# Dealing the weight conversion out as 6, 10, 9 and 7 pieces over the first four units of a gated attention and MLP kernel

## The chip, the core and the metric

The kernel runs on one core of one Trainium2 chip. The metric is device time in microseconds (us) for one execution. The engines are named TensorE (PE in the profile, with PEld for its weight loads), VectorE (DVE), ScalarE (ACT), GpSimd (POOL) and SyncE (SP, which issues the transfers). Each engine works through its own instructions strictly in order. An instruction that must wait for another engine holds up everything behind it on its own engine.

## What is computed

The first half is a gated linear recurrence over 4 batches, 8 heads, 768 tokens and a head size of 48. The second half is an MLP with a quick GELU over the 3072 tokens, with 384 features and 2048 hidden columns. The MLP weights arrive as 64-bit floats.

```python
f = 1.0 / (1.0 + np.exp(-f_logit))
for t in range(S):
    state = f[:, :, t, :, None] * state + np.einsum('bhd,bhe->bhde', k[:, :, t], v[:, :, t])
    y[:, :, t] = np.einsum('bhd,bhde->bhe', q[:, :, t], state)
x = y.transpose(0, 2, 1, 3).reshape(B * S, H * D)
h = x @ w_in
out = (h * (1.0 / (1.0 + np.exp(-1.702 * h)))) @ w_out
```

## The kernel before

**Units.** The tokens are cut into twelve units of 256 tokens, 0 to 11. `attention(n)` returns the parts of unit n's recurrence. In units 0 to 2 there are six levels ("W" parts, `level`), two transposes of the keys ("T", `turn_k`), the chain of states ("S", lines 511 to 544), and a last part that multiplies by the states and sends the result to the MLP's layout (line 546 on, `to_x`). That last part of a unit is put at the head of the next unit's first part, so it lies at the seam between the two. Three "begin" parts ("B", "K") of the next unit are put between them.

**One level.** On TensorE a level has 32 score products (`sc`, L384) and then, for the level before, 32 products with the values (`y`, L448). VectorE follows with two multiplications that carry keys and queries to the next level in place in X (L436, L437) and one masked copy of the scores out of PSUM to A (L410). ScalarE copies the keys of the next level aside (`Kc`, L423). The next level's scores need A copied (they reuse its PSUM tile), Kc copied and X carried on; VectorE's multiplication needs the scores to have been read. So one level waits for the one before, from TensorE to VectorE and back. From unit 3 on, two levels are done at once (L439 in place of L436 and L437), and VectorE turns the inputs (L327) where TensorE (`t`, L339) does it for units 0 to 2. GpSimd multiplies the gates together (`tot`, L376).

**The chain of states.** At the end of a unit VectorE computes four states, one after the other (`st`, L538, L540, L543). The products of the last part (`y`, L563) need them, and the next unit's first scores need the last L543, since it reads the same PSUM tile.

**Weights.** Lines 146 to 241 turn the 64-bit weights into 32-bit ones. There are 32 pieces of 128 by 384 numbers, in 16 pairs. Pairs come in groups of four: two of `w_in` and then two of `w_out`, which serve four of the sixteen blocks of 128 hidden columns. A pair is fetched by SyncE into one of three buffers (`bits`, L180). It is begun by two ScalarE instructions (`a`, L208). Then it takes ten VectorE instructions, two each of L223, L219, L226, L227 and L228; the two pieces of a pair alternate, and L228 writes the finished weight. Each `convert()` issues one of these ten; a new pair is begun when at most five are left over. When a pair is finished, the fetch of the third pair after it is issued, in the order of SyncE's queue at that moment.

**What sets the order.** `merge` walks through a unit's parts and puts two things between them: MLP work for TensorE (`fill`), shared out by columns, and conversion instructions for VectorE, shared out by `pieces`. A call with `pieces=8` issues 8 times NOP = 40 of them, in proportion to weights of the parts: three for each W and T and one for each B in units 0 and 1, three for W and S and one for T and B from unit 2 on. `by=0.7` in the fourth call brings them all within the first 70% of the weights. Four conversions are issued before unit 0, so 4 + 5 (8 + 10 + 8 + 6) are 164, and there are 160 to do. `some` holds an MLP block back in the order while the pieces it needs are not yet finished in program order.

```python
n_ops = min(int(pieces * NOP * at_ops / (by * total_ops)), pieces * NOP) - ops
while fill and done < end and fill[0][2] <= ready:
```

Unit 0 has no MLP work. Instead of it `keep_up` (L809) gives TensorE products that nobody reads: two in each of the first three levels of unit 0, and three in the first level of unit 1. They are in both kernels. Unit 1 has the MLP of unit 0 beside it, unit 2 that of units 0 and 1, unit 3 that of units 0 to 2. The order on all engines is the program's up to `fill_order.close()`; behind it that holds for TensorE only.

**MLP blocks.** `h` (L727) is the first matrix product. ScalarE's sigmoid `sg` (L732) and VectorE's `g` (L733) follow it, and `o` (L755) is the second product. It is added up over four groups by L791 (ScalarE) and L793 (VectorE). From unit 3 on, `mlp_unit` uses sums of weights (`T`, L622) in the second product (L704). All MLP products, transposes (`t` L339, `tkn` L505) and turned values (`tv` L284) share four PSUM tiles named `mm`.

Of the kernel before, what the change touches and what calls it, by code (L numbers as in the profile page):

```python
# [23 lines left out]
def kernel(  # L24
# [206 lines left out]
    def convert():  # L231

        if state["begin"] < len(pairs) and len(todo) <= NOP:
            begin_pair(state["begin"])
            state["begin"] += 1
        if todo and todo[0]:
            todo.pop(0)()
        if todo and todo[0] is None:
            todo.pop(0)
            state["done"] += 2  # L240
            fetch_weights()
# [556 lines left out]
    def mlp_blocks(*blocks):  # L798

        hs, os = zip(*(mlp_block(n, r) for n, r in blocks))  # L800
        return sum(hs, []) + sum(os, [])
# [10 lines left out]
    LAG = 18 * DM  # L812

    def parts_of(n):

        parts = list(units[n][1])
        _, inter = parts.pop()
        if n:
            kind, scores = parts[0]
            _, ahead = units[n - 1][1][-1]  # L820
            parts[0] = kind, lambda: (ahead(), scores())
        if n < N_TURN:

            def with_v(l):
                kind, fn = parts[l]
                return kind, lambda: (fn(), load_vl(n, l) if n == 0 or l else None, keep_up(2 * (n == 0 and l < 3) or 3 * (n == 1 and l == 0)))
            parts[:NL] = [with_v(l) for l in range(NL)]
        if n + 1 < NALL:
            begin_f, begin, begin_k, begin_gates = units[n + 1][0]
            i = len(parts)  # L830
            if n + 1 < N_FILL:

                parts.append(("K", lambda: (begin_k(), begin_gates(), load_vl(n + 1, 0) if n + 1 < N_TURN else None)))
                parts.insert(i - 4, ("B", begin))
                parts.insert(i - 5, ("B", begin_f))
            else:
                kind, states = parts.pop()
                parts += [("B", begin_k), (kind, lambda: (states(), begin_gates()))]
                parts.insert(i - 3, ("B", lambda: (begin_f(), begin())))
        else:  # L840
            parts.append(("W", inter))
        return parts

    def merge(n, fill, columns, share, pieces=0, hold=0, by=1.0, chores=()):

        parts = parts_of(n)
        total = sum(share(kind) for kind, _ in parts)
        converting = {"W": 3, "T": 3, "B": 1} if n < N_FILL - 1 else {"W": 3, "V": 4, "S": 3, "T": 1, "B": 1}  # L850
        total_ops = sum(converting.get(kind, 0) for kind, _ in parts)
        held = sum(share(kind) for kind, _ in parts[:hold])
        at = at_ops = done = ops = 0
        for kind, fn in parts:
            ready = state["done"]
            fn()
            for chore in chores[:2]:
                chore()
            chores = chores[2:]
            at += share(kind)  # L860
            at_ops += converting.get(kind, 0)
            n_ops = min(int(pieces * NOP * at_ops / (by * total_ops)), pieces * NOP) - ops
            ops += n_ops
            first, n_columns = done, max(0, columns * (at - held) / (total - held) - done)

            def some(end):
                nonlocal done
                while fill and done < end and fill[0][2] <= ready:
                    w, emit, _ = fill.pop(0)
                    emit()  # L870
                    done += w
            for i in range(n_ops):
                some(first + n_columns * i / n_ops)
                convert()
            some(first + n_columns)
# [4 lines left out]
    UNIT = NFF * NK * U + U // P * NFF * DM  # L880
# [12 lines left out]
        load_raw(1, j)  # L893
    load_vn(1)
    fill = []
    merge(0, fill, 0, steady, 8)
    fill += mlp_blocks((0, 0)) + mlp_blocks((0, 1))
    merge(1, fill, UNIT // 2 - LAG // 2, steady, 10, hold=1)
    fill += mlp_blocks((1, 0), (1, 1)) + mlp_blocks((0, 2), (1, 2))
    merge(2, fill, UNIT, steady, 8)  # L900
    fill += mlp_blocks((2, 0), (2, 1)) + mlp_blocks((2, 2), (0, 3)) + mlp_blocks((1, 3), (2, 3))
    merge(3, fill, 3 * UNIT // 2 - LAG // 2, steady, 6, by=0.7)
    fill_order.close()
    for n in range(3, NALL):
        fill += mlp_unit(n)
# [33 lines left out]
```

## Time and profile before

| what | value |
|---|---|
| median of 8 runs | 659.58 us (657.49 to 662.04) |
| the profiled execution's own time | 656.95 us |
| its span | 654.8 us |
| mean granted TensorE clock | 0.997 |
| TensorE busy | 635.4 us, 97% |
| VectorE busy | 444.9 us, 68% |
| ScalarE busy | 229.7 us, 35% |
| GpSimd busy | 54.7 us, 8% |

Times in the trace are counted from the start of the span. Unit 0's levels begin at 13.1 us, unit 1's first scores are at 44.64 us, unit 2's at 85.20 us, unit 3's at 142.13 us. From 212 us on, units 4 to 11 and the rest of the MLP run with no conversion. A tenth of busy time on the page is one slice of 16.4 us. Where an instruction's duration overlaps the next one on the same engine, the distance from start to start is what it costs.

### The profile page before, as it was taken

The page shows a single profiled execution, that of the slowest core. Times are in us where ns is not written, and L with a number is a line of the kernel's source. Part 1 is how long each engine was busy: PE and PEld are TensorE (multiplying, and loading weights), DVE is VectorE, ACT ScalarE, POOL GpSimd, SP SyncE. Part 2 cuts the span into 40 slices and gives each one's busy share as a digit, 9 for nine tenths or more (in the row PEclk, how much of TensorE's full clock was granted, in tenths as well). Part 3 has the DMA queues.
Part 4 walks back from the last instruction along what each step waited for, and adds up shares of the span by engine and source line. Part 5 has one row for each costly group of instructions (what it writes and reads, how often), then busy time and mean ns, then how long its engine had stood idle before and what let it go on. Part 6 is the DMA issues. An engine that isn't in the chain of part 4 may idle for free.

```text
span 654.8 us, 20407 instructions
## 1 busy us (share of the span) xinstructions
PE 635.4 (97%) x8964; PEld 544.8 (83%) x8964; DVE 444.9 (68%) x802; ACT 229.7 (35%) x477; POOL 54.7 (8%) x116
## 2 busy tenths in 40 slices
PE   6979999999999999999999999999999999999997
PEld 5656767767678689989989989989989989989997
DVE  2999878788787658658558558558559557553571
ACT  3464443233224324324324324324324333222120
POOL 3020020010001002002002002002002002000000
PEclk9999999989999999999999999999999999999999
DMA  8887975384034535514614615605604202101000
GB/s 191 225 203 181 226 167 134 96 208 84 25 81 133 155 85 121 153 39 119 162 30 121 158 35 123 164 26 127 160 27 106 65 25 63 38 2 26 25 1 24
DMA packets 67554, 67.67 MB, mean 103 GB/s; under 512 B 30410, under 2 KB 61290, under 8 KB 67466
## 3 DMA queue, kind: packets, MB, share of 16 engines
q1 hardware_dynamic: 67466, 66.38, 40.7%
q8 instruction: 70, 1.15, 0.8%
q14 instruction: 18, 0.15, 0.1%
HBM read 56.92 MB, written 8.65 MB: 100 GB/s over the span
## 4 chain that ended last, share of the span: by engine, by line
PE 86%; DVE 8%; ACT 2%; issue 1%; DMA 1%; SPq 0%; DVEq 0%; ACTq 0%
PE h L727 37%; PE o_Y L704 8%; PE o L755 7%; PE o_X L704 7%; PE o_Z L704 7%; PE sc L384 5%; PE y L448 5%; PE o_W L704 4%; PE t L339 2%; PE y L563 2%; PE sc L523 1%; PE tkn L505 1%; DVE s L219 1%; DMA xT<-yT 1%; DVE A L410 1%
## 5 line engine op out<-in xcount | busy, mean ns | idle before, releaser
L727 PE MATMUL h<-xT,w_in 128*128 128x256 f32 (+1 forms) x1152 | 259.4, 381 | 4.1 <-DMA xT<-yT 2.5
L727 PEld LDWEIGHTS h<-xT,w_in 128*128 128x128 f32 x1152 | 216.0, 190 | 36.3 <-issue 3.1
L733 DVE TENSOR_TENSOR g<-h,sg 128x256 f32<-128x256 f32 (+1 forms) x192 | 80.9, 423 | 97.5 <-ACT sg L732 95.1
L732 ACT ACTIVATE sg<-h 128x256 f32<-128x256 f32 (+1 forms) x192 | 73.3, 383 | 191.8 <-PE h L727 187.2
L423 ACT COPY Kc<-X 128x512 f32<-128x512 f32 x69 | 46.2, 669 | 120.8 <-DVE X L439 84.8
L755 PE MATMUL o<-w_out,g 128*128 128x384 f32 x192 | 67.4, 499 | 0.0
L439 DVE TENSOR_TENSOR X<-X,tot 128x1024 f32<-128x1024 f32 x45 | 55.1, 1224 | 15.3 <-PE sc L384 10.2
L755 PEld LDWEIGHTS o<-w_out,g 128*128 128x128 f32 x192 | 35.8, 193 | 23.3 <-issue 2.4
L704 PE MATMUL o_X<-w_out,g 128*128 128x192 f32 x288 | 51.9, 329 | 0.0
L704 PE MATMUL o_Y<-T,S 128*128 128x192 f32 x288 | 51.2, 331 | 0.0
L704 PEld LDWEIGHTS o_Y<-T,S 128*128 128x128 f32 x288 | 46.5, 190 | 2.5 <-DVE u L679 1.2
L704 PEld LDWEIGHTS o_X<-w_out,g 128*128 128x128 f32 x288 | 47.3, 190 | 0.8
L410 DVE TENSOR_TENSOR A<-sc,masks 128x512 f32<-128x512 f32 x72 | 46.8, 680 | 0.0
L448 PE MATMUL y<-A,vl 64*48 64x64 f32 x2304 | 41.2, 217 | 0.2
L376 POOL TENSOR_TENSOR tot<-F 128x512 f32<-128x512 f32 x12 | 12.5, 1040 | 327.5 <-DVE st L540 327.5
L448 PEld LDWEIGHTS y<-A,vl 64*48 64x48 f32 x2304 | 36.2, 120 | 3.7 <-issue 3.3
L327 DVE STREAM_TRANSPOSE X<-raw 128x1024 f32<-128x1024 f32 x18 | 36.7, 2039 | 2.4 <-PE y L563 2.0
L571 ACT COPY yT<-y 48x512 f32<-48x512 f32 x48 | 27.8, 580 | 13.6 <-PE y L563 13.0
L384 PEld LDWEIGHTS sc<-X,Kc 48*64 48x64 f32 x1344 | 24.4, 136 | 9.0 <-ACT vl L288 3.1
L384 PE MATMUL sc<-X,Kc 48*64 48x64 f32 x1344 | 28.6, 222 | 2.2 <-DVE A L410 1.9
L376 POOL TENSOR_TENSOR tot<-tot 128x256 f32<-128x256 f32 (+4 forms) x60 | 27.4, 457 | 4.7
L704 PE MATMUL o_Z<-w_out,g 128*128 128x192 f32 x144 | 26.6, 332 | 0.0
(93 smaller groups left out, 660.9 us busy)
## 6 DMA issues: line engine op xcount, KB each, us to landing
vl<-v_tok SPq DMA_DIRECT2D x60, 192.0 KB, 2.8
bits<-in_moe_w_out_dram SPq DMA_DIRECT2D x8, 768.0 KB, 9.9
bits<-in_moe_w_in_dram SPq DMA_DIRECT2D x8, 576.0 KB, 7.5
v_tok<-in_v_dram SPq DMA_DIRECT2D x10, 384.0 KB, 4.3
vn<-v_tok SPq DMA_DIRECT2D x10, 384.0 KB, 6.6
xT<-yT SPq DMA_DIRECT2D x24, 144.0 KB, 2.8
raw<-in_f_logit_dram SPq DMA_DIRECT2D x18, 192.0 KB, 4.2
raw<-in_q_dram SPq DMA_DIRECT2D x18, 192.0 KB, 4.1
```

What stands on the lines that cost most here:

```text
L327: nc.vector.transpose(out.rearrange("p (a i j) -> p a j i", a=NP, j=R), raw[:, j].rearrange("p a (j d) -> p (a j) d", j=R)[:, :, :32],)
L376: nc.gpsimd.tensor_tensor(tn, t2[:, :, 0], t2[:, :, 1], ALU.mult)
L384: nc.tensor.matmul(out[g * HS:(g + 1) * HS, h, a, :], lhsT=lhs(h, a * U + g * G), rhs=rhs(h, a * U + g * G), start=True, stop=True,)
L410: nc.vector.tensor_tensor(A[:, :, c:c + w].rearrange("p h (x t) -> p h x t", t=64), t["sc"][:, :, c:c + w].rearrange("p h (x t) -> p h x t ...
L423: nc.scalar.copy(c.rearrange("p (n m) -> p n m", m=m), X[:, j, :NA].rearrange("p (n two m) -> p n two m", two=2, m=m)[:, :, hf, :],)
L439: nc.vector.tensor_tensor(qk, qk, by, ALU.mult)
L448: nc.tensor.matmul(dst(h, g, a), lhsT=vls[n, u][g * 64:(g + 1) * 64, (2 * a + h) * D:(2 * a + h + 1) * D], rhs=A(h, g, a), start=(start an ...
L704: nc.tensor.matmul(t[bank], lhsT=lhs(f), rhs=rhs(f), start=(new and f == 0), stop=(f == HF - 1), skip_group_check=True,)
L727: nc.tensor.matmul(ph, lhsT=w_in[:, c, ff * P:(ff + 1) * P], rhs=xTs[n][:, c, :], start=(c == 0), stop=(c == NK - 1))
L732: nc.scalar.activation(sg, ph, AF.Sigmoid, scale=1.702)
L733: nc.vector.tensor_tensor(g[ff // FG][:, ff % FG, :], ph, sg, ALU.mult)
L755: nc.tensor.matmul(t["po"], lhsT=g[ff // FG][:, ff % FG, tt * P:(tt + 1) * P], rhs=w_out[:, ff, :], start=(ff == ffs[0]), stop=(ff == ffs[ ...
```

## The change

The `pieces` of three of four calls of `merge` change, for units 0, 2 and 3. Units 0 to 3 were dealt 8, 10, 8 and 6 pieces; they are dealt 6, 10, 9 and 7 after it. Both add up to 32. The products that nobody reads are not touched.

```diff
-    merge(0, fill, 0, steady, 8)
+    merge(0, fill, 0, steady, 6)
     fill += mlp_blocks((0, 0)) + mlp_blocks((0, 1))
     merge(1, fill, UNIT // 2 - LAG // 2, steady, 10, hold=1)
     fill += mlp_blocks((1, 0), (1, 1)) + mlp_blocks((0, 2), (1, 2))
-    merge(2, fill, UNIT, steady, 8)
+    merge(2, fill, UNIT, steady, 9)
     fill += mlp_blocks((2, 0), (2, 1)) + mlp_blocks((2, 2), (0, 3)) + mlp_blocks((1, 3), (2, 3))
-    merge(3, fill, 3 * UNIT // 2 - LAG // 2, steady, 6, by=0.7)
+    merge(3, fill, 3 * UNIT // 2 - LAG // 2, steady, 7, by=0.7)
```

In the instruction streams, TensorE's order is the same in both kernels. On VectorE, ten conversions leave unit 0 and go to the units behind it. As ten are exactly one pair, unit 1 has the same kinds of instruction in the same places, each for the pair before. Unit 2 takes five more and unit 3 five more. ScalarE's L208 and SyncE's fetches move with the pairs.

## Prediction

> **What bounds the kernel now.** First the page: which engine is full, and where in time.
>
> ```profile
> PE 635.4 (97%) x8964; PEld 544.8 (83%) x8964; DVE 444.9 (68%) x802; ACT 229.7 (35%) x477; POOL 54.7 (8%) x116
> ...
> PE   6979999999999999999999999999999999999997
> ...
> DVE  2999878788787658658558558558559557553571
> ```
>
> TensorE is full from about 50 us on, and its work is not changed, so only its waits can be won or lost. They lie in the first slices, where VectorE is at nine tenths. Then the same by stage: unit 0's levels, unit 1, unit 2, unit 3, and the long rest.
>
> ```profile
> 13.00:45.00 32.00, 27.15 (x677) 18.62 (x681) 30.61 (x69) 16.20 (x32) 3.72 (x8) 1.00 0.94 234
> 45.00:86.00 41.00, 39.17 (x731) 27.95 (x723) 36.68 (x85) 21.06 (x44) 4.39 (x10) 1.00 0.83 199
> 86.00:142.00 56.00, 52.37 (x648) 38.17 (x648) 43.33 (x86) 19.33 (x40) 3.27 (x8) 1.00 0.57 138
> 142.00:212.00 70.00, 69.49 (x802) 52.77 (x806) 55.87 (x99) 23.01 (x48) 6.51 (x14) 0.98 0.37 89
> ```
>
> The columns are stretch, length, busy time of TensorE, its weight loads, VectorE, ScalarE and GpSimd, granted clock, DMA share, GB/s. In unit 0 VectorE works 30.61 of 32 us while TensorE is free for 4.85 us. In unit 1 TensorE is free for 1.8 us, in unit 2 for 3.6, in unit 3 for 0.5. So unit 0 is VectorE's stage, and the stages behind it are TensorE's. The chain of work that ended last says the same of unit 0:
>
> ```profile
> 28.41 0.55 DVE w_in L228
> 28.95 0.54 DVE a L223 x2
> ...
> 29.88 0.55 DVE s L219
> 30.43 0.60 DVE X L436
> 31.03 0.60 DVE X L437
> 31.63 0.60 DVE A L410
> 32.23 0.54 DVE a L226 x2
> 32.77 0.94 DVE a L227 x2
> ...
> 40.88 0.94 DVE s L219 x2
> 41.81 0.28 DVE st L538
> ```
>
> From 14.27 to 43.72 us it stays on VectorE, and the conversions (L219 to L228) are links of it like the level's own three. What TensorE waits for there, in the order of its waits, are copies and states behind those conversions:
>
> ```profile
> PE sc L384 <- DVE A L410: 1.1, 2, 0.6
> PE tkn L505 <- DVE X L436: 1.1, 1, 1.1
> ...
> PE y L563 <- DVE st L538: 0.8, 1, 0.8
> PE y L563 <- DVE st L543: 0.5, 1, 0.5
> ```
>
> **Unit 0 loses ten conversions.** Start to start, two L223 take 0.54 us, two L219 0.94, two L226 0.54, two L227 0.94, two L228 0.94: a pair costs VectorE 3.90 us. Before, 4, 5, 4, 7, 6 and 14 conversions stand behind the six levels; after, 3, 3, 4, 5, 4 and 11. A level's own three take 1.81. I follow VectorE's queue, and let each level wait for TensorE's scores where these are now later. L436 of the six levels starts at 15.35, 18.65, 22.39, 25.67, 30.35 and 34.56 us, and the states at 41.72. Level 1: one L227 less (0.47), so 18.2. Level 2: the queue is free at 21.4, but its scores can't start before 21.13, since ScalarE's Kc stands behind a pair's L208 that waited for its transfer until 19.45; they take 0.69, so 21.85. Level 3: the scores at 24.49 stand directly behind TensorE's unread products, which don't move; they end at 25.18, so 25.2. Level 4: scores at 28.11 as now, queue free at 27.0 + 1.95 = 28.95. Level 5: queue 30.76 + 1.48 = 32.25, but TensorE starts the scores at 31.75 (turns of raw end there), so 32.47. Then 1.81, and eleven conversions of 4.37: the states begin at 38.67 in place of 41.72. Of the 3.90 removed, 3.05 arrives; the rest becomes waits of VectorE for scores. TensorE has to be there too: its keys' transposes go from 35.39 to 33.63, the second half of L523 from 38.11 to 36.4 (ScalarE's kn copies are no longer parted by an L208 pair), turns and tv follow without a gap to 39.5, before the state it needs second (39.9). The scores of unit 1 stand behind the last L543 and go from 44.64 to 41.6. **Minus 3.05 us.** Bounds: TensorE's waits from 13.8 us to unit 1's first scores add up to 4.5, so no more than 3.9 (the queue) can go; if the products and turns of TensorE were the limit alone, 42.13 to 39.5 is 2.6.
>
> **Unit 1: nothing.** Each conversion is of the same kind in the same place, one pair earlier in the list; each stall shifts along, such as the 1.05 us for xT at 51.03. The weights come one pair later, and must be there. The tightest: blocks 6 and 7 of w_out, read by o at 85.84, are written where the next pair is now, at 79.15 to 80.5: 5 us to spare. Had they been late, o would wait for as much.
>
> **Unit 2: five conversions more, and an order that changes on ScalarE.** In the levels VectorE has gaps of 0.4 to 1.6 us, and one conversion more in each (0.27 to 0.47) lies in them; TensorE's work (5.4 us a level) covers it. At the end it does not:
>
> ```profile
> 127.91 1.06 ACT L332 ACTIVATE F<-F 128x1024 f32<-128x1024 f32 x1 [2.51 <-DVE F L327]
> 129.13 0.57 ACT L506 COPY kn<-tkn 128x512 f32<-128x512 f32 x1
> 129.76 2.86 PE L727 MATMUL h<-xT,w_in 128*128 128x256 f32 x12 [1.32 <-ACT kn L506]
> ```
>
> In the new order an L208 pair stands directly behind this L332, ahead of sg and kn (it stood behind both kn copies). It costs ScalarE 0.93, kn frees its PSUM tile that much later, and TensorE's h goes from 129.76 to 130.69: a wait of 2.25 in place of 1.32. Then g, the turn of the keys (L327, 132.43 to about 132.98), L439 and the last g follow 0.55 later on VectorE, and the states with them (138.83 to 139.4). Today TensorE waits there for states (0.20, 0.47, 0.21), so of its 0.93 a part is taken up, and unit 3's first scores lie behind the last L543: **plus 0.55**, between 0.1 (g not held up) and 0.93 (TensorE's delay whole). Blocks 10 and 11 of w_out, read by o at 135.05 and 135.4, are now written behind the L327s, at about 131.4 and 132.3: 3 us to spare.
>
> **Unit 3: five more.** VectorE has 14 us free of 70. The two sums T, which now hold up g and give TensorE a wait of 0.32 at 155.74, go behind four more g: **minus 0.3**, between minus 0.32 and plus 0.3 (another g late by one conversion). The last weights are written at about 186 and read at 193.
>
> **Transfers.** On SyncE pair 4's fetch goes behind unit 2's raw gates, pair 6 behind xT, v and the first vl, pair 11 behind the next unit's xT, 14 behind raw q, 15 behind xT. Their L208 stand a pair later in ScalarE's order too. The shortest: pair 6 takes the slot of pair 7, issued 56.03 and begun at 62.14 with no wait, so nothing; raw and xT move ahead. If that cover failed, ScalarE's queue (sg, Kc) would stop for the rest of a transfer (median 7.5 to 9.9 us).
>
> **Sum.** Minus 3.05, plus 0.55, minus 0.3: minus 2.8, or 656.95 to 654.15 for the profiled execution, span 652.0. That execution is below all eight runs (2.6 under the median), so the difference goes to the median: 659.58 to **656.8**.
>
> **The clock.** In the profile the granted clock is 1.00 but for one stretch: 0.72 at 142, 0.50 at 143 and 144, 0.57 at 145. It stretched 16 o products from 5.43 to 6.41 and two sets of scores by 0.73, so it cost 1.7 us. It came after 3 us in which TensorE's waits were 0.20, 0.47 and 0.21 long; the wait of 1.32 at 128.4 brought none. So where a stretch falls can't be read from one wait's length: a new 2.25 us wait may bring one (plus 1.7), a shorter gap at the states may spare this one (minus 1.7). I take neither and keep both for the range. The Trainium skill, "TensorE: Matmul & The Clock Gate", Part 1, says that an idle window of about 3.4 us halves the clock, and the table at its end asks for no gaps over about 3 us. By that rule 2.25 us is harmless and the sum stays at minus 2.8; the stretch at 142 does not fit that reading, since no gap near it was over 0.5.
>
> **Rivals.** (A) As summed, 656.8, by itself 655.4 to 657.6. Speaking for it: the chain in unit 0 is without a break VectorE's. (B) Most of it is lost on the way: unit 0 gives TensorE's 2.6, and unit 2 takes the whole 0.93, with 0.3 more in unit 3: minus 1.4, 658.2. For it: no unit behind unit 0 is free of VectorE's waits. Against it: the states, VectorE's own chain, end the unit. (C) Slower: the clock. If the longer wait before h in unit 2 brings low stretches at 1.7 each, 2.8 is used up by the second, and three more than before give 656.8 + 5.1 = 661.9. For it: this stretch is the kernel's only one with a low clock. Against it: it needs three, and unit 0, with its shorter waits, has a clock of 1.00. (D) The change doesn't do what its name says: the unread products are in both kernels and TensorE's order is the same; then it still moves the conversions, so this changes no number.
>
> **How the numbers follow.** A 0.62, B 0.28, C 0.10. About 0.3% (2 us) is what a measurement of this kernel can tell from no change, so faster is below 657.6 and slower above 661.6. A falls mostly below (0.58) and a little between (0.04); of B 0.05 is faster with a spared stretch, and 0.23 between; of C 0.08 is slower, 0.02 between. Faster 0.63, same 0.29, slower 0.08. Low end: all 3.90 less 0.1 and 0.3 more, with half a spared stretch, minus 5.0: 654.6. High end: B with a stretch more, minus 1.4 + 1.7, and the scatter between runs of 0.5: 660.4.
>
> **What would show it.** Right: states of unit 0 near 38.7, unit 1's scores near 41.6 and unit 2's near 82.1, h waiting about 2.2 in unit 2, unit 3's scores near 139.6. Wrong: if VectorE idles in unit 0 for more than 1 us, if o waits for w_out (L228), or if the clock falls in another place or more often.

## The result and the profile after

The changed kernel takes 655.07 us (median of 20 runs), and the kernel before 657.95 us (55 runs beside it). The ratio is that of the means, without one slow execution of 663.60 us: 0.9962, with a 95% interval of 0.9946 to 0.9977. So the change is worth 2.5 us, between 1.5 and 3.6. The sum was minus 2.8 us. The time was forecast at 656.8; 1.6 us of the difference lie in the median of before, 659.58 in the runs shown then and 657.95 here.

The profile after is not of a typical execution: it took 659.96 us by itself, 4.9 above its median, and its span is 658.0 us. So it shows where the kernel can lose, and a third profile of the same kernel, further down, shows the common case. The page of the changed kernel, its busy times and its slices, with the granted clock as the last row:

```profile
PE 637.7 (97%) x8964; PEld 546.5 (83%) x8964; DVE 445.0 (68%) x802; ACT 230.1 (35%) x477; POOL 55.3 (8%) x116
...
PE   6989989999999999999999999999999999999997
...
DVE  2989857779886757657657658658558557553571
...
PEclk9999989989999999999999999999999999999999
```

TensorE is 2.3 us busier with the same 8964 instructions, and the clock row has an 8 in slices 6 and 9 where before has one, in slice 9. So some of its work ran slower. Here are the stretches between the first scores of the units, with the columns as before:

```profile
13.47:41.24 27.77, 25.65 (x654) 17.98 (x658) 26.73 (x59) 14.91 (x29) 3.52 (x8) 1.00 0.92 219
41.24:82.94 41.70, 39.06 (x723) 27.69 (x716) 36.10 (x83) 21.11 (x42) 4.01 (x9) 1.00 0.83 201
82.94:145.83 62.89, 57.57 (x689) 42.09 (x681) 45.49 (x92) 20.92 (x44) 4.14 (x9) 0.92 0.58 137
145.83:214.20 68.37, 66.82 (x740) 50.42 (x743) 57.60 (x104) 22.25 (x47) 6.77 (x14) 1.00 0.37 94
```

Before, first scores are at 13.13, 44.64, 85.20, 142.13 and 211.09 us, so its units are 31.51, 40.56, 56.93 and 68.96 us long. After, unit 0 begins 0.47 later and is 3.87 shorter (27.64 from its first scores at 13.60); unit 1 is 1.14 longer, unit 2 is 5.96 longer, unit 3 is 0.57 shorter, and the rest is the same within 0.1. That adds up to the 3.2 us by which this span is longer than that of before.

Unit 0 did what was expected of it, and more. The chain that ended last, at the end of unit 0, still runs over VectorE and its conversions:

```profile
34.51 0.54 DVE a L226 x2
35.05 0.94 DVE a L227 x2
...
36.92 0.54 DVE a L223 x2
37.46 0.94 DVE s L219 x2
38.40 0.28 DVE st L538
```

The states come 24.71 us behind the first scores, and 28.59 before. That is 3.88 less, and the ten conversions were 3.90.

Unit 2 took it all away in this execution. First TensorE's own rows, in which the bracket tells the wait ahead of a row and what ended it:

```profile
92.88 8.46 PE L727 MATMUL h<-xT,w_in 128*128 128x256 f32 x24 [2.79 <-DMA xT<-yT]
```

Then the rows of ScalarE and TensorE at the end of its levels:

```profile
130.03 1.06 ACT L332 ACTIVATE F<-F 128x1024 f32<-128x1024 f32 x1 [2.50 <-DVE F L327]
131.00 0.98 ACT L208 ACTIVATE a<-bits 128x384 f32<-128x384 f32 x2
...
132.15 0.57 ACT L506 COPY kn<-tkn 128x512 f32<-128x512 f32 x1
...
132.77 4.54 PE L727 MATMUL h<-xT,w_in 128*128 128x256 f32 x12 [2.20 <-ACT kn L506]
```

The L208 pair stands between L332 and kn, and h waits 2.20 us, as forecast (2.25). But 12 products h took 4.54 us, where before they took 2.86, and the 24 behind the wait for xT took 8.46. Before, at full clock, this row was:

```profile
93.79 5.42 PE L727 MATMUL h<-xT,w_in 128*128 128x256 f32 x24 [1.44 <-DMA xT<-yT]
```

Behind both waits the granted clock of this execution fell to 0.5. So of unit 2's 5.96 us, TensorE's waits are 1.56: 1.35 more for xT, 0.88 more for kn, and 0.67 less for the states, since TensorE itself came late to them. Its busy time is 4.40 more (57.57 for 53.17): 3.04 and 1.68 from the two stretches, less 0.3 elsewhere.

### The profile page after: what moved, and what is told of

Same layout as the page of the kernel before. It is cut to its first block, busy times and chain, and to the rows that moved or that the text cites. A ratio compares the mean times of both kernels' runs of the same rounds, so it can differ in the third digit from the quotient of the medians.

```text
span 658.0 us, 20406 instructions
## 1 busy us (share of the span) xinstructions
PE 637.7 (97%) x8964; PEld 546.5 (83%) x8964; DVE 445.0 (68%) x802; ACT 230.1 (35%) x477; POOL 55.3 (8%) x116
## 4 chain that ended last, share of the span: by engine, by line
PE 83%; DVE 7%; DMA 6%; SPq 2%; issue 1%; ACT 1%; DVEq 0%; ACTq 0%
PE h L727 37%; PE o L755 7%; PE o_X L704 7%; PE o_Y L704 7%; PE o_Z L704 7%; PE sc L384 5%; PE y L448 4%; PE o_W L704 4%; DMA vn<-v_tok 2%; DMA bits<-in_moe_w_in_dram 2%; PE y L563 2%; PE sc L523 1%; PE tkn L505 1%; DMA raw<-in_q_dram 1%; DMA xT<-yT 1%
## 5 line engine op out<-in xcount | busy, mean ns | idle before, releaser
L727 PE MATMUL h<-xT,w_in 128*128 128x256 f32 (+1 forms) x1152 | 264.1, 386 | 8.0 <-DMA xT<-yT 4.2
L727 PEld LDWEIGHTS h<-xT,w_in 128*128 128x128 f32 x1152 | 218.8, 193 | 42.2 <-issue 3.9
```

The source lines that it names most:

```text
L727: nc.tensor.matmul(ph, lhsT=w_in[:, c, ff * P:(ff + 1) * P], rhs=xTs[n][:, c, :], start=(c == 0), stop=(c == NK - 1))
```

## The experiments

The theory at this point: unit 0's gain arrives whole, and what is lost on the way is lost behind waits of TensorE, by the clock. The rivals: that the gain is lost because the units behind have no room for conversions, or that the clock is chance and has nothing to do with the waits.

### The changed kernel again

No edit. The kernel was profiled and timed in two more sessions, on two chips.

> The changed kernel once more, for a second profile beside the others. Theory (the gain is VectorE's shorter queue in unit 0, part of it given back behind it): ratio 0.994 to 0.998; from unit 0's first scores to unit 1's first scores 27.7 us where the kernel before takes 31.5. The first profile of the changed kernel has two stretches of low clock in unit 2 (at 92 to 98 and 132 to 137 us) that cost 4.7 us. If they belong to the changed kernel, they are here again in the same places; if they fall by chance, at most one is.

> The changed kernel a third time, on the chip of its neighbours here. If the deal is worth what the first measurement gave: ratio 0.996 +-0.002, unit 0 at 27.6 us when no stretch of low clock falls into it, and the wait for kn in unit 2 at 2.20 in every profile. If it is worth nothing and the scatter of the clock gave the first ratio: 0.998 to 1.001.

The first took 658.81 us beside 659.35 for before (ratio 0.9988, 0.9963 to 1.0014), the second 657.55 beside 659.32 (0.9979, 0.9949 to 1.001). Each interval overlaps that of the first result, and neither excludes no change. So the three sessions put the gain at 0.1 to 0.4%, each with its own uncertainty.

The profile of the second is the common case: span 653.2, units 28.30, 41.28, 58.07 and 68.38 us. TensorE's rows in unit 2:

```profile
91.75 5.42 PE L727 MATMUL h<-xT,w_in 128*128 128x256 f32 x24 [1.55 <-DMA xT<-yT]
...
128.62 4.54 PE L727 MATMUL h<-xT,w_in 128*128 128x256 f32 x12 [2.21 <-ACT kn L506]
```

The wait for xT is 1.55 here, and the 24 products behind it run at full clock. The wait for kn is the same 2.21, with the slow products behind it again. In the profile of the first repeat it is the other way round. The wait for xT is 2.85 with slow products behind it, the wait for kn brought none, and unit 0 was 33.32 us long:

```profile
14.13 3.19 PE L284 MATMUL tv<-vn,ident 128*64 128x384 f32 x4 [1.38 <-DMA vn<-in_v_dram]
17.26 1.63 PE L809 MATMUL idle<-masks,ident 128*128 128x384 f32 x4
...
96.44 6.86 PE L727 MATMUL h<-xT,w_in 128*128 128x256 f32 x24 [2.85 <-DMA xT<-yT]
...
134.73 2.86 PE L727 MATMUL h<-xT,w_in 128*128 128x256 f32 x12 [2.20 <-ACT kn L506]
```

There the first scores started at 12.05 us, and vn hadn't landed: 4 products tv took 3.19 us (0.88 after). The clock fell at 14 to 15 us in five of the fourteen profiles, those whose first scores started at 12.60 or sooner; none of the nine that started at 12.73 or later shows it. The states came 27.05 us behind the first scores here, 2.3 later than in the other two profiles. The rest of the 33.32 are two holes of TensorE, of 0.68 and 2.68 us, to which the section on the same cover in unit 1 comes back.

### The kernel before again

No edit; the kernel before was profiled once more.

> The kernel before, profiled a second time, as the measure of what scatters by itself between executions. If the stall of xT in unit 2 (1.44 us in the first profile, 2.79 and 2.85 in the two profiles of the change) belongs to the deal of the weights, it is 1.2 to 1.7 us here again, and unit 2 is 56.9 us +-0.5 long. If it is scatter of transfers, it lies anywhere between 1.0 and 2.9. The stretch of low clock at 142 us: if it goes with the order of the work it is here again; if it is chance it is somewhere else or missing.

Its span was 658.0, 3.2 us above its first profile. Unit 0 is 31.87 us long, unit 2 59.22:

```profile
95.74 5.49 PE L727 MATMUL h<-xT,w_in 128*128 128x256 f32 x17 [2.14 <-DMA xT<-yT]
```

The wait for xT is 2.14 us, and the clock is low at 95 to 99 us, not at 142; all 24 products took 7.00. So a long wait for xT with slow products behind it is not the change's own: it belongs to both kernels and comes and goes. SyncE's waits of the changed kernel (83 to 96 us) point to where it comes from:

```profile
SPq L592 <- ACT yT L571: 3.1, 1, 3.1
SPq L592 <- DMA vn<-v_tok: 1.6, 1, 1.6
```

The second part of xT is issued only when the earlier transfer vn has landed. That wait of SyncE was 1.6 us after and 0.6 in this profile; it does not show in the first profile of before, nor in the last one of the changed kernel, where TensorE waited 1.44 and 1.55. Ten profiles have that wait of TensorE with no work of ours put ahead of it. In six SyncE waited 0.6 to 1.6 for vn, and TensorE 2.14 to 2.85 for xT; in four it waited 0.5 or not at all, and TensorE 0.78 to 1.66. No run sets the transfer apart.

### The later part alone, and unit 1 in place of units 2 and 3

```diff
-    merge(0, fill, 0, steady, 6)
+    merge(0, fill, 0, steady, 8)
...
-    merge(3, fill, 3 * UNIT // 2 - LAG // 2, steady, 7, by=0.7)
+    merge(3, fill, 3 * UNIT // 2 - LAG // 2, steady, 5, by=0.7)
```

> 8, 10, 9, 5: unit 0 keeps its ten conversions, and unit 2 gets the five more of the change (unit 3 has one piece less than before). Theory: nothing is gained, since unit 0 is as before (31.5 us); the wait before h in unit 2 is 2.2 us in place of 1.3, because a pair's L208 stands behind L332 here too; time plus 0 to plus 1.5 us, ratio 1.000 to 1.002. Rival (the gain comes from the order of transfers and conversions in the later units, not from unit 0): minus 1.5 us or more.

```diff
-    merge(1, fill, UNIT // 2 - LAG // 2, steady, 10, hold=1)
+    merge(1, fill, UNIT // 2 - LAG // 2, steady, 12, hold=1)
...
-    merge(2, fill, UNIT, steady, 9)
+    merge(2, fill, UNIT, steady, 8)
...
-    merge(3, fill, 3 * UNIT // 2 - LAG // 2, steady, 7, by=0.7)
+    merge(3, fill, 3 * UNIT // 2 - LAG // 2, steady, 6, by=0.7)
```

> 6, 12, 8, 6: the ten conversions go to unit 1 and nothing changes behind it. Theory: unit 0 takes 27.7 us as in the change, but unit 1's VectorE goes from 36.7 to 40.6 us of 41, so unit 1's levels wait for it and unit 1 gets longer by 1 to 3.5 us; time minus 2.5 to plus 0.5. Rival (TensorE's MLP work covers the conversions in unit 1): unit 1 as long as before, minus 3 us or more.

The deal 8, 10, 9, 5 took 660.77 us (1.0015 of before, 0.999 to 1.004). Unit 0 was 31.50 long, and h in unit 2 had its wait of 2.20 with 12 slow products (4.54 us) as in the changed kernel. So the conversions in unit 2 bring nothing by themselves, and the gain needs the ten that leave unit 0.

The deal 6, 12, 8, 6 took 659.45 us (1.0002, 0.9974 to 1.003). Unit 0 was 27.62 and unit 1 45.52, 4.96 longer than before. TensorE's rows in unit 1 show what the unit lacked:

```profile
79.03 1.10 PE L523 MATMUL sc<-vn,kn 64*64 64x48 f32 x32 [2.52 <-ACT kn L506]
80.06 2.64 PE L727 MATMUL h<-xT,w_in 128*128 128x256 f32 x6
```

The wait for kn is 2.52 us, and behind it 6 products h take 2.64 us, where 6 take 1.46. That wait and the low clock at 79 to 83 us (about 1.7 us) are most of the 4.96. So where the ten conversions go decides what they are worth: in this profile unit 1 gives back more than the 3.9 us that unit 0 gains.

### The order in unit 2 put back

```diff
+        if n == 2:
+            converting["B"] = 0
```

No conversion then stands behind a begin part of unit 2; the deal stays 6, 10, 9, 7. The L208 pair that stood between L332 and kn is not behind kn now, as in the kernel before, but ahead of L332 (at 126.50 us in this profile), and the next pair comes at 141.77. Where two expectations further down say "put back behind kn", this order is meant.

> The changed kernel, with unit 2's begin parts given no conversions (the five are spread over its other parts), so that the pair's L208 stands ahead of unit 2's L332 and not between it and the kn copies. Theory: the wait before h falls from 2.2 to about 1.3 us, and the time is 0.3 to 0.9 us below the changed kernel's. Rival (that wait is taken up by the states behind it): the wait falls and the time stays within 0.2 us. If the wait brings the low clock, the stretch at 132 to 137 us goes with it, and 1.7 us more.

It took 658.32 us (0.997 of before, 0.9944 to 0.9996), in the same session as the first repeat of the changed kernel, 658.81. ScalarE and TensorE at the end of unit 2's levels:

```profile
131.65 1.06 ACT L332 ACTIVATE F<-F 128x1024 f32<-128x1024 f32 x1 [2.51 <-DVE F L327]
132.61 0.37 ACT L732 ACTIVATE sg<-h 128x256 f32<-128x256 f32 x1
132.88 0.58 ACT L506 COPY kn<-tkn 128x512 f32<-128x512 f32 x1
...
133.51 2.21 PE L727 MATMUL h<-xT,w_in 128*128 128x256 f32 x9 [1.32 <-ACT kn L506]
```

The wait is back to 1.32, the products run at full speed, and unit 2 is 57.40 long although it waited 2.24 for xT. That the L208 pair made the longer wait is shown. The 0.5 us between the two medians are less than these runs can tell.

This profile also had the low clock in unit 0, at 15 to 22 us, and there VectorE does wait for scores in unit 0:

```profile
21.20 0.69 DVE L437 TENSOR_TENSOR X<-X,tot 128x512 f32<-128x512 f32 x1 [2.23 <-PE sc L384]
```

### Unread products at the long wait

Two `keep_up` products (four instructions of TensorE, 1.56 us) at the end of unit 2's level 1, ahead of the h that waits for xT; on top of the version of the last section, and alone on the kernel before.

```diff
+        if n == 2:
+            kind1, fn1 = parts[1]
+            parts[1] = kind1, lambda: (fn1(), keep_up(2))
```

> The deal of the change with the two L208 pairs of unit 2 put back behind kn, and two unread products more at the end of unit 2's level 1, ahead of the h that waits for xT. Theory (a long wait of TensorE before h is what brings the low clock): the wait for xT shrinks by what the products take (about 0.5 us), there is no low clock between 90 and 105 us, and the time is 0.1 to 0.3% below that of the version with the order alone, near 0.994 of the kernel before. Rival (the low clock comes on TensorE's load, not on a gap): the products change nothing of where it falls, and the time stays at 0.997.

> The kernel before, with its deal of 8, 10, 8 and 6, and only the two unread products (four of TensorE's instructions, about 1.5 us) at the end of unit 2's level 1 added, ahead of the h that waits for xT (1.44 and 2.14 us in the two profiles of before). Theory (the gain of 0.7% in the run that has the deal and the cover is the sum of two things): the wait for xT shrinks to 0.1 to 0.7 us, unit 0 keeps its 31.5 to 31.9 us, there is no low clock at 94 to 100 us, and the time is 0.1 to 0.2% below the kernel before. Rival (the cover is the whole gain): 0.7% below it here too. Second rival (the products only put h off): 0 to 0.2% above it.

With the deal and the order it took 654.97 us, 0.9927 of before (0.9895 to 0.9959), and all seven executions lay between 654.35 and 656.38. In unit 2:

```profile
90.59 1.56 PE L809 MATMUL idle<-masks,ident 128*128 128x384 f32 x4
93.26 5.42 PE L727 MATMUL h<-xT,w_in 128*128 128x256 f32 x24 [1.10 <-DMA xT<-yT]
```

Alone on the kernel before it took 658.38 us, 0.9984 (0.9963 to 1.0005), with the wait for xT at 0.54:

```profile
93.62 1.56 PE L809 MATMUL idle<-masks,ident 128*128 128x384 f32 x4
95.72 5.42 PE L727 MATMUL h<-xT,w_in 128*128 128x256 f32 x24 [0.54 <-DMA xT<-yT]
```

So the rival that the cover is the whole gain falls, since the intervals of the two do not overlap.

The granted clock of every execution shows what the cover does. In the fourteen profiles each stretch of low clock lasts about 3.4 us, or two or three times that, at 0.5. One of 3.4 us takes the mean of an execution from 1.000 to 0.997, and most means come in such steps: 1.000, 0.997, 0.995, 0.992, 0.990. So the mean tells about how many there were. In this table an execution counts as full when its mean clock is 0.999 or more, and as low when it is below 0.9965, which is some two stretches or more. The last column has the full ones of the kernel before in the same sessions.

| kernel | executions | full | low | mean time of the full ones, us | before |
|---|---|---|---|---|---|
| before (three sessions) | 86 | 24 | 37 | 657.9 | |
| 6, 10, 9, 7, the first result | 20 | 6 | 5 | 654.2 | not on record |
| 6, 10, 9, 7, the two repeats | 24 | 3 | 15 | 656.3 | 657.9 |
| with the order | 12 | 1 | 9 | 654.5 | 657.8 |
| with the order and the cover | 7 | 4 | 0 | 654.7 | 657.7 |
| cover alone on before | 12 | 7 | 2 | 658.0 | 658.1 |
| no unread products in unit 0 | 10 | 0 | 10 | none | 657.7 |

Within one session the change is worth 1.6 to 1.7 us at full clock, from only three executions of it, and 3.0 with the order and the cover, from four. The 654.2 of the first result can't be used that way: the clocks of before are not on record in that session, and its median there was 657.95, where it was 658.73 to 659.35 in the others. The cover is worth nothing at full clock (658.0 beside 658.1); with it the low executions are rarer, none of 7 and 2 of 12, where before has 11 of 22 and 12 of 29 in the same sessions.

### The same cover in unit 1 too

```diff
-        if n == 2:
+        if n in (1, 2):
             kind1, fn1 = parts[1]
```

> The version with the order and the cover in unit 2, and the same two unread products at the end of unit 1's level 1 too, ahead of its h, which waits for xT by 1.33 to 1.55 us. Theory (a cover is free where TensorE waits for a transfer for as long): the wait goes to about 0, unit 1 keeps its 41.0 to 41.5 us, and the time is that of the version with one cover, 0.993 of the kernel before. Rival (the products also put off what stands behind them in unit 1, which has no room): unit 1 is 0.3 to 1.0 us longer and the time 0.05 to 0.15% above that version.

It took 655.59 us, 0.9947 (0.9925 to 0.9969). The wait for xT in unit 1 fell only to 0.86, unit 1 was 41.86 long against 41.46 with one cover, and the full executions (7 of 12) have a mean of 655.4. So the rival's size fits better than the theory's, but the intervals of the two versions overlap. The profile has another kind of hole, at the end of unit 0:

```profile
38.56 1.02 PE L523 MATMUL sc<-vn,kn 64*64 64x48 f32 x54 [1.77 <-issue]
...
43.87 0.21 PE L563 MATMUL y<-X,ident 48*48 48x1 f32 x2 [1.03 <-issue]
```

TensorE stands for 1.77 and 1.03 us in the middle of a run of products of one kind, and waited for nothing that its waits name. Unit 0 is 30.76 long here, with no low clock in it. The transfers tell what it lacked. Besides the kernel's data the page has one more queue:

```profile
q8 instruction: 70, 1.15, 0.8%
```

These 70 transfers carry 16 KB of program code each. TensorE's products and weight loads are 17,928, which is 256 for each transfer, while the other engines have far fewer instructions. There are 17 holes put down to issue between 35 and 50 us, in ten of the fourteen profiles. Each of them ends 1.2 to 1.7 us after one of these transfers has ended (here they ended at 36.99 and 42.62). And each stands at one of three places of TensorE's order, behind 1217, 1473 or 1729 of its instructions in the trace, which lie 256 apart. That holds whatever row stands there, also in the kernel of the next section, which has fewer products in unit 0. So TensorE stood there without its next block of code. The faster deal runs into this at the end of unit 0. In the first profile of before, TensorE gets to the place behind 1473 at 43.8 us, 2.7 after the last such transfer ended, and there is no hole; in that of the changed kernel it gets there at 40.5, 0.9 after, and goes on at 40.9. Why a block comes when it does was not tested.

### Without the unread products of unit 0

```diff
-keep_up(2 * (n == 0 and l < 3) or 3 * (n == 1 and l == 0))
+keep_up(3 * (n == 1 and l == 0))
```

> The changed kernel without the unread products of TensorE in unit 0's first three levels (they compute nothing that is read). Theory (unit 0 is set by VectorE's queue alone): the states stay within 0.3 us of 24.3 us behind the first scores, and unit 0 stays at 27.6 us; TensorE's waits grow by the 1 to 2 us of the products. Rival (the prediction's: scores behind the products hold VectorE up by 0.85 us in unit 0): the unit gets shorter by 0.3 to 0.85 us. Third: the longer waits bring a stretch of low clock within unit 0, and the unit is 0.5 to 2 us longer.

It took 659.59 us, 1.0005 of before (0.998 to 1.0031), and all ten executions are low. The rival falls: nothing got shorter. From the first L436 of unit 0 to the states VectorE takes 22.53 us here and 22.48 in the changed kernel, with the products or without. In the profile unit 0 is 32.34 us long. The states are 25.34 behind the first scores, 0.6 later than in the changed kernel, as the first L436 is, and then a hole of the kind of the last section stands on the path:

```profile
14.27 0.83 PE L284 MATMUL tv<-vn,ident 128*64 128x384 f32 x2 [0.97 <-DMA vn<-in_v_dram]
15.68 1.54 PE L284 MATMUL tv<-vn,ident 128*64 128x384 f32 x2 [0.57 <-DMA vn<-in_v_dram]
...
44.74 0.26 PE L563 MATMUL y<-X,st 48*48 48x64 f32 x2 [3.43 <-issue]
```

The clock is low from 15 to 22 us and again behind the hole. So the products that nobody reads cost VectorE's queue nothing in the changed kernel, and without them the clock was low in every execution.

### Unit 3's pairs spread wider

```diff
-    merge(3, fill, 3 * UNIT // 2 - LAG // 2, steady, 7, by=0.7)
+    merge(3, fill, 3 * UNIT // 2 - LAG // 2, steady, 7, by=0.85)
```

This is on top of the version with the order in unit 2 put back.

> The deal of the change with the two L208 pairs of unit 2 put back behind kn, and unit 3's seven pairs spread over a longer part of that unit (0.85 for 0.7), so that one conversion less stands in front of the two sums of L793. Theory (h of unit 3 waits 1.55 us for those sums, which stand behind VectorE's conversions): the wait falls by 0.4 to 0.6 us to about 1.0, unit 3 is 67.9 us in place of 68.4, and the time is 0.1% below that of the version with the order alone, near 0.996 of the kernel before. Rival (the sums stand behind g and the scan, not behind conversions): the wait stays at 1.5 to 1.7, unit 3 at 68.4.

It took 656.76 us, 0.9962 (0.993 to 0.9994). The wait fell by what was expected, but unit 3 was 69.27 us long, not 67.9. TensorE's rows:

```profile
152.36 2.00 PE L727 MATMUL h<-xT,w_in 128*128 128x256 f32 x8 [1.06 <-DVE sum L793]
```

```profile
194.05 2.20 PE L755 MATMUL o<-w_out,g 128*128 128x384 f32 x6 [0.63 <-DVE w_out L228]
```

Now o waits 0.63 for its weights, which are written later, and another h waits 0.38 for xT at 148. One wait was exchanged for two, 0.5 us more in all; the rest of the 0.9 by which the unit is longer was not traced.

### Ten conversions more out of unit 0

```diff
-    merge(0, fill, 0, steady, 6)
+    merge(0, fill, 0, steady, 4)
...
-    merge(2, fill, UNIT, steady, 9)
+    merge(2, fill, UNIT, steady, 10)
...
-    merge(3, fill, 3 * UNIT // 2 - LAG // 2, steady, 7, by=0.7)
+    merge(3, fill, 3 * UNIT // 2 - LAG // 2, steady, 8, by=0.7)
```

This is on top of the order and the cover in unit 2.

> The version with the order and the cover in unit 2, but with pairs dealt 4, 10, 10, 8: ten conversions more leave unit 0. That also changes TensorE's order where blocks of h and o are held back until their weights are there. Theory (VectorE's queue still sets unit 0, until TensorE's own work does): TensorE's products and turns bind before all of the next 3.9 us has come, so unit 0 falls from 27.6 to between 25.0 and 26.4 us; units 1 to 3 take 1 to 3 us more, as weights are late or VectorE's gaps are used up, and the time is between 0.991 and 0.997 of the kernel before. Rival: the unit falls by the whole 3.9 to 23.8 us. Third: it doesn't fall at all, since TensorE already sets it.

It took 667.06 us, 1.0108 (1.0064 to 1.0152). It is best held against the profile with the cover, since both started at 12.6 us and had the low clock in unit 0, from about 15 us on. The states come 24.88 us behind the first scores, 26.53 there: 1.65 of the 3.90 arrive. VectorE's rows in unit 0 show where the others went:

```profile
19.40 0.69 DVE L437 TENSOR_TENSOR X<-X,tot 128x512 f32<-128x512 f32 x1 [1.42 <-PE sc L384]
...
22.76 0.69 DVE L437 TENSOR_TENSOR X<-X,tot 128x512 f32<-128x512 f32 x1 [0.51 <-PE sc L384]
...
26.11 0.69 DVE L437 TENSOR_TENSOR X<-X,tot 128x512 f32<-128x512 f32 x1 [0.53 <-PE sc L384]
...
33.35 0.69 DVE L437 TENSOR_TENSOR X<-X,tot 128x512 f32<-128x512 f32 x1 [0.72 <-PE sc L384]
```

Those four, with 0.25 in the level between, are 3.43 us; 1.12 of them it had with the cover too, so 2.31 are new, and 3.90 less 2.31 is 1.59. This is the point at which VectorE's queue alone no longer sets the states: the scores hold it up. Nor does the unit get what the states gained. It is 29.35 us long, and 29.45 with the cover: TensorE goes from its turned values to the last products without a wait for a state, 26.98 us behind the first scores (27.80 with the cover), and then stands 1.25 us for its next block of code. And the units behind pay for the deal. In unit 2 TensorE ran out of work (64 products o there with six pieces in unit 0, 48 with four, as blocks are held back for their weights) and waited for the states:

```profile
143.36 0.45 PE L563 MATMUL y<-X,st 48*48 48x64 f32 x4 [5.17 <-DVE st L543]
```

Unit 2 is 61.60 long, 3.85 more than with six pieces and the cover; unit 3 is 70.70, 2.3 more, and the rest 447.99, 4.2 more. The stretches of low clock are longer too, six times 3.4 us in this profile and one with the cover. The expectation was right that TensorE would bind before all of the 3.9 us had come; it put unit 0 at 25.0 to 26.4 us, which is nowhere near 29.35, and missed what the units behind would lose.

## Why the prediction was right, and where it was not

**The sum.** Minus 2.8 was forecast, and minus 2.5, 0.8 and 1.4 us were measured in three sessions, each of these uncertain by 1 to 2 us. The sign stands. The first measurement fits rival A, and the two repeats fall short of it. That the first came so near is partly luck: two terms were wrong in opposite directions, unit 0's was too small and the clock's was put at nothing.

**Unit 0, minus 3.05.** The step "let each level wait for TensorE's scores" put 0.85 us of waits into VectorE's queue that did not come. In the four profiles with this unit undisturbed (the result's, the third of the changed kernel, the deal with twelve in unit 1, and unit 3's pairs spread wider) the states come 24.71 to 24.73 us behind the first scores; in the four with eight pieces 28.59 to 28.76. All of the 3.90 arrived. The working gives 25.54. It had the L436 of levels 2 to 5 start at 8.72, 12.07, 15.82 and 19.34 behind the first scores; they started at 8.26, 11.54, 15.28 and 18.56. The queue had been followed rightly (level 1 forecast at 5.07, measured 5.05), but the wait for the scores was put in front of L436. Where VectorE does wait for them, the rows show it in front of L437, the second multiplication, 0.60 us later, and by then the scores have been read. The kernel tells why: L436 carries the keys, which the scores read from their copy Kc, and L437 the queries, which the scores read in X. The bound of 2.6 from TensorE's turns did not bind either. What the working did not have are the holes before TensorE's next block of code. They are 0.90 us in unit 0 of the third profile of the changed kernel and 3.36 in that of the first repeat.

**Unit 1, nothing.** The kernels with eight pieces in unit 0 have 40.56 to 42.03 us there in four profiles, those with six and ten 40.99 to 41.86 in eight. The step stands, within that scatter (means 41.1 and 41.4).

**Unit 2, plus 0.55.** This step held, in cause and size, where the clock stayed up behind the wait. The wait for kn behind the L208 pair was 2.20, and it goes back to 1.32 when the pair does. In the profile of the first repeat no slow products stand behind it. The unit is 60.33 long there. Its wait for xT is 1.41 longer than in the first profile of before, and the 24 products behind that wait took 1.44 more; without these two it is 57.48, and 0.55 more than the 56.93 of before. A part of the longer wait is taken up by the waits for the states, as the step said: they are 0.88 us before and 0.62 in the first repeat:

```profile
139.69 0.32 PE L563 MATMUL y<-X,st 48*48 48x64 f32 x4 [0.20 <-DVE st L543]
140.48 1.45 PE L563 MATMUL y<-X,st 48*48 48x64 f32 x60 [0.47 <-DVE st L543]
142.13 0.92 PE L384 MATMUL sc<-Qc,Kc 48*64 48x64 f32 x32 [0.21 <-DVE st L543]
```

```profile
145.12 1.44 PE L563 MATMUL y<-X,st 48*48 48x64 f32 x60 [0.41 <-DVE st L543]
146.77 0.69 PE L384 MATMUL sc<-Qc,Kc 48*64 48x64 f32 x32 [0.21 <-DVE st L543]
```

With the order put back, the same reckoning gives 57.40 less 0.80 for xT, 56.60, so the pair behind L332 cost 0.9 us. Where 12 products ran slow behind the wait, the unit lost more. In the third profile of the changed kernel it is 58.07 long, plus 1.14: TensorE's busy time is 54.26 for 53.17 us, and it came so late that its waits for the states are gone.

**Unit 3, minus 0.3.** It is 68.38 to 68.39 long where it was 68.96 and 68.60, so minus 0.2 to 0.6. But the step's reason does not hold: the wait for g went, and in its place h waits 1.4 to 1.6 us for the sums of L793:

```profile
156.64 3.72 PE L727 MATMUL h<-xT,w_in 128*128 128x256 f32 x16 [1.55 <-DVE sum L793]
```

Those stand there in the repeats too, and spreading the pairs wider to shorten the wait gained nothing.

**The clock.** "I take neither" was the step that failed most, and the prediction's own sign for it came: the clock fell in another place and more often. The waits of 2.20 or 2.21 for kn were followed by a low clock in four of five profiles (not in the first repeat), at up to 1.7 us before what later slack takes up. And the price of 1.7 is not what a stretch costs in every place: unit 3 of the kernel before is 68.96 us long with the stretch at 142 and 68.60 in its second profile without it, where the waits for L793 and g are 0.63 and 0.51 in place of the one of 0.32. There 0.4 was to be won, not 1.7.

The Trainium skill, "TensorE: Matmul & The Clock Gate", Part 1, has the clock fall after an idle window of about 3.4 us; read that way, a gap of 2.2 us is harmless. The rows decide against that reading: of the 18 waits of TensorE of 2.1 us or more in the fourteen profiles, from unit 0's first scores on, 14 had a low clock with or behind them, and of 47 between 1.0 and 1.9 us only one did. Two of the 18 were as long as such a window (3.43 and 5.17 us). So the rival that the clock has nothing to do with the waits does not stand. But waits are not all of it: six of the 21 stretches came with no wait of 1.0 us or more.

**The rivals.** B (most is lost on the way) had the wrong reason, since VectorE's queue in unit 0 lost nothing; but the two repeats, at minus 0.8 and 1.4, lie about where it put the time. C had the right mechanism, and one execution shows it: the profiled one of 659.96 us has two stretches in unit 2, one of them twice as long as the other and at 3.0 us, not 1.7. Three more in every execution it did not come to. D changes no number, as was said: the unread products are in both kernels, though in the run without them the clock was low in all ten executions.

What stays open: why the gain was smaller in the two repeats. Low executions were 8 and 7 of 12 there, and 5 of 20 in the first result, beside 14 of 35 and 12 of 29 for before in the same sessions as the repeats. An estimate from the mean clocks makes this 2.2 and 2.0 stretches of 3.4 us for each execution, where before has 1.5 and 1.6. The executions of before at 0.992, three stretches, take 661.5 us on average and the full ones 657.9, so one costs some 1.2 us, and the more frequent low clock 0.9 and 0.5 us. That is a part of it. At full clock the change was worth 1.6 to 1.7 there and not 2.8. The holes before TensorE's next block of code may be in that: they are 1.4 us on average in the eight profiles with six pieces in unit 0 and the unread products, and 0.7 in the four with eight. No run shows that either comes from the deal and not from chance.

## What to carry to other kernels

When a queue is followed instruction by instruction, put each wait at the instruction that has it in the trace, not at the first one of the step: here the 0.6 us between L436 and L437 were the difference between a loss of 0.85 and none. Moving work out of the engine that sets a stage pays whole until something else sets it, and costs whole where the stage that takes it has no room: the ten conversions cost unit 1 about 5 us where it took them all, with a stretch of low clock in it, and five of them cost unit 2 some 0.55 us without such a stretch and 1.14 with one. Where a wait of some 2 us of TensorE can't be taken away, work that nobody needs in that place can be worth having for the clock behind it, and the evidence for that is in the clock of many executions, not in one profile.

The version with the order and the cover (654.97 us, 0.9927 of before) is the best one measured. That it also beats the changed kernel was not measured side by side: the intervals against before (0.9895 to 0.9959, and 0.9946 to 0.9977) overlap a little.

## What was not expected of the hardware

- A stretch of low clock has one length. In the fourteen profiles there are 21: 16 last about 3.4 us, four 6.8 and one 10.2, all at 0.5. One of 3.4 us costs 1.7 in most places (12 products h 4.54 for 2.86, 24 in 7.11 for 5.42 with unit 3's pairs spread wider), one of 6.8 up to 3.0 (24 in 8.46). It also came where no wait was long: at 142 to 143 us in two profiles, behind waits under 0.5 us.
- TensorE's holes at the end of unit 0 and the start of unit 1, 0.2 to 3.4 us long, are waits for its own program code, with both deals, though no line of the waits names it. The transfer engines are 0.50 to 0.86 busy from 35 to 50 us, and less in the profiles with the longest holes.
- Executions of one program on one chip differ by 6 to 8 us (before: 656.40 to 664.19 in one session). That is more than twice what this change is worth, so a single profile of each kernel, 654.8 against 658.0 us of span, had the sign wrong.
